# Quads 5 to 23 of an attention kernel: the turning of q and k moved from a transposing transfer to 32x32 blocks on VectorE and plain transfers

## The chip, the cores and the metric

The kernel runs on one core of a Trainium2 chip. The metric is the device time of one execution in microseconds (us). Two runs of the kernel before took 372.81 and 373.34 us, a median of 373.07 us.

## The reference

Attention with a squared ReLU in place of a softmax, and then a two-layer network on its output:

```python
# q, k, v: (8, 12, 448, 64): batch, heads, sequence S, head width D
scores = (1 / np.sqrt(D)) * np.matmul(q, k.transpose(0, 1, 3, 2))
attn = np.maximum(scores, 0.0) ** 2 / S
attn_out = np.matmul(attn, v)
x = attn_out.transpose(0, 2, 1, 3).reshape(B * S, H * D)     # 3584 x 768
h = x @ w_in                                                 # 768 -> 2048
g = np.maximum(h, 0.0) + alpha * np.minimum(h, 0.0)
out = g @ w_out                                              # 2048 -> 768, float32
```

Inputs and the output are float32 in HBM; the kernel computes its products in bf16 and accumulates in float32.

## The kernel before, in words

**Tiles.** Four heads of one batch element make a quad, so there are 3 quads in each of 8 batch elements, 24 in all (n = 0 to 23). The 448 rows of a head are held as 64 partitions of 7 rows (row = 7*pp + j). `load_qk` (L111) brings q and k of a quad by one transfer each, issued on GpSimd's queue (POOL), which casts to bf16: partitions are (head of a pair, pp), and the free dimension holds two pairs, 7 rows and 64 columns. `load_v` (L120) does the same for v. Three buffers hold raw q and raw k, six hold v.

**Turning.** The scores contract over the 64 columns, so these must come to lie on partitions. Quads 0 to 4 are turned on TensorE by `turn_pe` (L175). Quads 5 to 23 are turned by `turn_dma` (L188): two copies (L195), on ScalarE (ACT) or VectorE (DVE) by the letter that the plan gives, reorder q and k into a tile `perm`, and one transposing transfer, issued on SyncE's queue (SP, L197), writes the tile `T`. In quads 5, 7 and 8 a part of `w_mix` serves as `perm`, since it is not yet filled. There is one other `perm` buffer and four `T` buffers.

**Scores.** `score_mm` (L203) makes the scores of one quad and one j: four matmuls of 64x64 tiles (two row groups r, two column groups c), each with 448 moving columns, into a pair of the 8 PSUM banks. `relu` (L214, on ACT at L218 or DVE at L220) brings them to SBUF, `square` (L223, ACT at L229 or DVE at L231) squares them, `attnv` (L233) multiplies with v in 28 matmuls of 64x64 tiles (L241), and its result goes to `xT` (L253 or L255).

**The network.** `f1_mm` (L273) makes one of 16 units of the first layer for one batch element: six matmuls of 448 columns (L275) into one bank. `f1_out` (L279) lets ACT write `neg` (L281, two buffers) and DVE write `gT` from `neg` and the bank (L282). The second layer is made in `f2` (L290) or, for pairs of row blocks, in the class `Pair`, whose seven products p1 to p7 (L335) take mixed weights `w_mix` (made by DVE at L313) and mixed activations `S` (DVE, L331). DVE adds up results of these (L340), and results are stored by transfers on SP (L291); six `o` buffers hold them.

**Order.** Nothing is scheduled by a planner: the plan is a string of words written out by hand, one call after the other, which each engine then follows in order. `cA` or `cD` makes one score step with its relu on ACT or DVE; `s0D` squares; `v` is attnv; `f` is a unit of the first layer; `p5` is a product of a pair; `dnX` turns quad n with its copies on engine X; `ln` is `land(n)`; `Lqn` loads q and k of a quad; `nX` is `prepare` (L409): turn quad n, `land(n)`, load q and k of quad n+2 and v of quad n+1. Quads 5 to 10 are turned by `d` words, 11 to 23 by `n` words (`n` alone means ACT). By the letters, quads 5, 6, 7, 8, 12, 15, 18 and 20 are copied on DVE, the other eleven on ACT.

`land` (L417) is one copy of a single element of `T[n]` on POOL. As POOL's queue runs in order, the loads behind it are not issued before `T[n]` has landed.

The engines meet at semaphores only. SP's queue holds the transposing transfers and the stores of results in the plan's order; a transfer that waits holds up those behind it.

Of the kernel before, what the change touches and what calls it, by code (L numbers as in the profile page):

```python
# [11 lines left out]
BF16 = mybir.dt.bfloat16  # L12
# [2 lines left out]

PP = 64
NJ = 7


@with_exitstack  # L20
def kernel(
# [10 lines left out]
    nc = tc.nc  # L32
    B, H, S, D = q.shape
    d_model, d_ff = moe_w_in.shape
    assert H * D == d_model and S == PP * NJ and D == 64 and H % 4 == 0 and B % 2 == 0
    NG = H // 4
# [7 lines left out]
    ctx.enter_context(tc.manual_schedule())  # L44
    singles = ctx.enter_context(tc.tile_pool(name="singles", bufs=1))
    raw_pool = ctx.enter_context(tc.tile_pool(name="raw", bufs=3))
    v_pool = ctx.enter_context(tc.tile_pool(name="v", bufs=6))
    perm_pool = ctx.enter_context(tc.tile_pool(name="perm", bufs=1))
    T_pool = ctx.enter_context(tc.tile_pool(name="T", bufs=4))
    rl_pool = ctx.enter_context(tc.tile_pool(name="rl", bufs=6))  # L50
    at_pool = ctx.enter_context(tc.tile_pool(name="at", bufs=10))
    xT_pool = ctx.enter_context(tc.tile_pool(name="xT", bufs=2))
    neg_pool = ctx.enter_context(tc.tile_pool(name="neg", bufs=2))
    o_pool = ctx.enter_context(tc.tile_pool(name="o", bufs=6))
    u_pool = ctx.enter_context(tc.tile_pool(name="u", bufs=2))
    S_pool = ctx.enter_context(tc.tile_pool(name="S", bufs=4))
    ps_pool = ctx.enter_context(tc.tile_pool(name="ps", bufs=1, space=bass.MemoryType.PSUM))
# [9 lines left out]
    landed = singles.tile([1, 1], BF16)  # L67
# [12 lines left out]
    def take_pair():  # L80
        lo = min((0, 2, 4, 6), key=lambda i: (max(taken[i], taken[i + 1]), i))
        take(lo, 2)
        return psum[:, lo:lo + 2]
# [25 lines left out]
    raw, vraw = {}, {}  # L109

    def load_qk(n, names="qk"):  # L111
        b, g = divmod(n, NG)
        for name in names:
            src = q if name == "q" else k
            t = raw_pool.tile([128, 2, NJ, D], BF16, tag=name, name=f"{name}raw")
            flat = src[b].rearrange("(m two) (pp j) d -> (two pp) m (j d)", two=2, j=NJ)
            nc.gpsimd.dma_start(out=t.rearrange("p m j d -> p m (j d)"), in_=flat[:, 2 * g:2 * g + 2])
            raw[(n, name)] = t

    def load_v(n):  # L120
        b, g = divmod(n, NG)
        t = v_pool.tile([128, 2, NJ, D], BF16, tag="v", name="vraw")
        flat = v[b].rearrange("(m two) (pp j) d -> (two pp) m (j d)", two=2, j=NJ)
        nc.gpsimd.dma_start(out=t.rearrange("p m j d -> p m (j d)"), in_=flat[:, 2 * g:2 * g + 2])
# [12 lines left out]
    def load_w_out(h, lo=0, hi=KF, step=4):  # L137
        for lo in range(lo, hi, step):
            nc.gpsimd.dma_start(out=w_out_sb[:, lo:lo + step, COLS[h][0]:COLS[h][1]], in_=w_out_v[:, lo:lo + step, COLS[h][0]:COLS[h][1]])

    FIRST = 4
    flat0 = {name: src[0].rearrange("(m two) (pp j) d -> (two pp) m (j d)", two=2, j=NJ)[:, :2]
             for name, src in (("q", q), ("k", k))}
# [10 lines left out]
    for lo, hi, eng in ((0, 4, nc.sync), (4, NJ, nc.scalar)):  # L154
        t = o_pool.tile([128, 2, (hi - lo) * D], F32, tag="o", name=f"qfirst{lo}")
# [10 lines left out]

    warm(31)
    load_qk(1)
    load_v(0)
    load_qk(2)  # L170
    load_v(1)


    T = {}
# [13 lines left out]
    def turn_dma(n, eng="A"):  # L188
        if n in (5, 7, 8):
            w = w_mix[2 + n % 2].rearrange("p k c -> p (k c)")[:, :4 * NJ * D]  # L190
            p = w.rearrange("p (a j s d) -> p a j s d", a=2, j=NJ, s=2)
        else:
            p = perm_pool.tile([128, 2, NJ, 2, D], BF16, tag="perm", name="perm")
        for i, name in enumerate("qk"):
            (nc.vector.tensor_copy if eng == "D" else nc.scalar.copy)(p[:, i], raw.pop((n, name)).rearrange("p s j d -> p j s d"))  # L195
        t = T_pool.tile([128, 2, NJ, 128], BF16, tag="T", name="T")
        nc.sync.dma_start_transpose(out=t.rearrange("p a j c -> p (a j) c"),  # L197
                                    in_=p.rearrange("p a j s d -> p (a j s d)"))
        T[n] = t


    att, xT = {}, {}
# [1 line left out]
    def score_mm(n, j):  # L204
        ps = take_pair()
        t = T[n]
        for r in range(2):
            for c in range(2):
                nc.tensor.matmul(ps[64 * c:64 * c + 64, r, :S],  # L209
                                 t[64 * r:64 * r + 64, 1, j, 64 * c:64 * c + 64],  # L210
                                 t[64 * r:64 * r + 64, 0, :, 64 * c:64 * c + 64],
                                 start=True, stop=True)
        return ps

    def relu(ps, eng):
# [45 lines left out]
    def chunk(eng):  # L261
        if stream:
            n, j = stream.pop(0)
            late.append((n, j, relu(score_mm(n, j), eng)))
# [143 lines left out]
    def prepare(n, eng="A"):  # L408
        if n < NQ:  # L409
            turn_dma(n, eng)  # L410
            land(n)
        if n + 2 < NQ:
            load_qk(n + 2)
        if n + 1 < NQ:
            load_v(n + 1)

    def land(n):  # L417
        nc.gpsimd.tensor_copy(landed, T[n][:1, 0, 0, :1])  # L418

    class Walk:  # L420

# [11 lines left out]
        def step(self, w):  # L433
# [41 lines left out]
            elif c == "w":  # L475
                i, half = int(rest[0]), int(rest[1])
                weight_mix(i, 4 * half, 4 * half + 4)
            elif c == "g":
                f2(self.b // 2, int(rest[0]), int(rest[1]))
            elif c == "n":  # L480
                prepare(self.quad, rest or "A")
                self.quad += 1
            elif c == "x":
                cast0(int(rest[0]), int(rest[1]), rest[2])
            elif c == "t":
                turn_pe(int(rest[0]), ((rest[1], int(rest[2]), int(rest[3]), rest[4]),))
            elif c == "d":
                turn_dma(int(rest[:-1]), rest[-1])
            elif c == "l":
                land(int(rest))  # L490
            elif c == "L":
                n = [int(x) for x in rest[1:].split(",")]
                {"q": load_qk, "v": load_v, "i": load_w_in, "o": load_w_out}[rest[0]](*n)
            elif c == "i":
                warm(int(rest))
            elif c == "y":
                bank = min(range(8), key=lambda i: (taken[i], i))
                for _ in range(int(rest)):
                    nc.tensor.matmul(psum[:, bank, :128], idle, idle, start=True, stop=True)
            elif c == "z":  # L500
                two_queues.append(1)
            elif c == "b":
                nc.vector.tensor_scalar(beta_sb, alpha_sb, -1.0, 1.0, ALU.mult, ALU.add)
# [48 lines left out]
```

## Time and profile before

The profiled execution took 373.07 us, the same as the median; its span, from the first instruction to the last, is 371.3 us, so 1.8 us lie around it. The granted TensorE clock was 1.00 throughout.

| engine | busy us | share of the span | instructions |
|---|---|---|---|
| TensorE matmuls (PE) | 363.6 | 98% | 3105 |
| TensorE weight loads (PEld) | 197.5 | 53% | 3105 |
| VectorE (DVE) | 278.0 | 75% | 445 |
| ScalarE (ACT) | 274.7 | 74% | 406 |
| GpSimd (POOL) | 71.7 | 19% | 120 |

| transfers | number | us from issue to landing, median |
|---|---|---|
| transposing, from `perm` | 16 | 4.0 |
| transposing, from `w_mix` | 3 | 6.3 |
| loads of raw q / raw k / v, 224 KB each | 23 / 23 / 24 | 4.1 / 5.3 / 6.5 |
| stores of 96 KB on SP | 91 | 2.2 |

How to read it: an engine's busy time is the time in which at least one of its instructions ran. The page also has groups of instructions (line, engine, operation, output and inputs, count; then busy time, mean duration of one in ns, and the idle time just before them with what ended it), a chain of work followed back from the last instruction, and, when asked, a timeline (start in us, duration in us, engine, line, and how many instructions are merged in the row). A row that merges several instructions gives the time from the first one's start to the last one's end. Rows of DVE overlap by some 0.08 us, since one instruction begins while the one before it drains; so the step from start to start is 0.53 us where the duration is 0.61 us.

### The profile page before, as it was taken

Reading aid. Unit: us, or ns where it says so; the run is one execution under the profiler, and the core shown is the slowest. Engines: PE = TensorE matmul, PEld = TensorE weight load, DVE = VectorE, ACT = ScalarE, POOL = GpSimd, SP = SyncE. Lnnn points to the kernel's source line nnn. Section 1 sums busy time; section 2 is a strip of 40 time slices with the busy share of each in tenths; the row PEclk is TensorE's granted clock in tenths of the full one; section 3 lists DMA queues with packets and bytes.
Section 4 is the critical chain, followed back from the end, with each engine's and each line's share of the span. In section 5 each row is a group of like instructions: output and inputs, shape, how many; then the busy total and the mean of one; then the engine's idle time right before and its main releaser. Section 6 shows DMA issues by size and latency. Waiting matters only on the chain.

```text
span 371.3 us, 7894 instructions
## 1 busy us (share of the span) xinstructions
PE 363.6 (98%) x3105; PEld 197.5 (53%) x3105; DVE 278.0 (75%) x445; ACT 274.7 (74%) x406; POOL 71.7 (19%) x120
## 2 busy tenths in 40 slices
PE   8799999999999999999999999999999999999995
PEld 6454564444554565545555455554555455555563
DVE  3989988885968989566887768888749667856653
ACT  5998676877997678885997859967699866964400
POOL 8566150304211222022020220202200000000000
PEclk9999999999999999999999999999999999999999
DMA  9999989999999868455882659727646201220024
GB/s 143 188 203 202 199 135 191 153 160 167 180 171 150 123 96 163 92 89 90 160 144 64 99 80 168 144 56 121 111 89 134 49 2 43 65 65 0 0 64 108
DMA packets 73557, 43.29 MB, mean 117 GB/s; under 512 B 40368, under 2 KB 73008, under 8 KB 73520
## 3 DMA queue, kind: packets, MB, share of 16 engines
q0 software_dynamic: 27136, 22.58, 42.0%
q1 hardware_dynamic: 45712, 19.61, 25.9%
q10 hardware_dynamic: 672, 0.59, 0.5%
q8 instruction: 24, 0.39, 0.4%
q14 instruction: 13, 0.11, 0.1%
HBM read 45.62 MB, written 11.01 MB: 153 GB/s over the span
## 4 chain that ended last, share of the span: by engine, by line
PE 94%; DVE 2%; ACT 2%; issue 1%; ACTq 0%
PE psum L275 38%; PE psum L335 30%; PE psum L241 9%; PE psum L209 9%; PE psum L300 6%; PE psum L183 1%; PE psum L165 1%; DVE gT L282 1%; ACT rl L218 1%; ACT xT L253 1%; ACT neg L281 1%; DVE w_mix L195 1%; DVE T L186 0%; DVE at L231 0%; DVE osb L340 0%
## 5 line engine op out<-in xcount | busy, mean ns | idle before, releaser
L275 PE MATMUL psum<-xT,w_in_sb 128*128 128x448 bf16 x768 | 150.4, 353 | 0.2 <-DVE gT L282 0.2
L282 DVE SCALAR_TENSOR_TENSOR gT<-neg,beta_sb,psum 128x448 bf16<-128x448 f32 x128 | 85.3, 679 | 43.4 <-ACT neg L281 42.1
L218 ACT ACTIVATE rl<-psum 128x896 bf16<-128x896 f32 x128 | 111.2, 925 | 6.7 <-PE psum L209 4.7
L275 PEld LDWEIGHTS <-w_in_sb 128*128 128x128 bf16 x768 | 73.4, 98 | 73.0 <-issue 6.8
L281 ACT ACTIVATE neg<-psum 128x448 f32<-128x448 f32 x128 | 68.5, 547 | 41.0 <-PE psum L275 32.7
L231 DVE TENSOR_TENSOR at<-rl 128x896 bf16<-128x896 bf16 x105 | 62.2, 620 | 0.5 <-ACT rl L218 0.2
L229 ACT ACTIVATE at<-rl 128x896 bf16<-128x896 bf16 x63 | 58.6, 952 | 0.3
L335 PEld LDWEIGHTS <-S 128*128 128x128 bf16 x384 | 36.7, 98 | 28.4 <-issue 5.3
L335 PE MATMUL psum<-w_mix,S 128*128 128x384 bf16 x288 | 49.8, 326 | 0.2
L220 DVE TENSOR_SCALAR rl<-psum 128x896 bf16<-128x896 f32 x40 | 43.2, 1086 | 8.7 <-PE psum L209 8.1
L209 PE MATMUL psum<-T 64*64 64x448 bf16 x672 | 45.9, 357 | 2.0 <-DVE T L186 1.0
L418 POOL COPY landed<-T 1x1 bf16<-1x1 bf16 x18 | 3.3, 181 | 206.1 <-DMA T<-perm 182.9
L335 PEld LDWEIGHTS <-gT 128*128 128x128 bf16 x296 | 28.3, 98 | 20.2 <-issue 1.8
L241 PE MATMUL psum<-at,vraw 64*64 64x448 bf16 x672 | 36.6, 350 | 0.0
L335 PE MATMUL psum<-w_out_sb,gT 128*128 128x384 bf16 x192 | 34.0, 326 | 0.0
L340 DVE TENSOR_TENSOR osb<-psum,u 128x384 f32<-128x384 f32 (+2 forms) x37 | 20.2, 547 | 12.6 <-PE psum L335 8.2
L209 PEld LDWEIGHTS <-T 64*64 64x64 bf16 x672 | 17.4, 105 | 22.7 <-issue 14.8
L241 PEld LDWEIGHTS <-vraw 64*64 64x64 bf16 x672 | 21.2, 106 | 11.9 <-issue 2.9
L300 PE MATMUL psum<-w_out_sb,gT 128*128 128x256 bf16 (+1 forms) x128 | 22.0, 326 | 0.1
L255 DVE TENSOR_SCALAR xT<-psum 128x448 bf16<-128x448 f32 x24 | 14.9, 622 | 8.9 <-PE psum L241 8.3
L253 ACT ACTIVATE xT<-psum 128x448 bf16<-128x448 f32 x24 | 13.3, 556 | 9.1 <-PE psum L241 8.7
L356 ACT COPY osb<-psum 128x384 f32<-128x384 f32 x12 | 5.8, 480 | 17.4 <-PE psum L335 17.4
(45 smaller groups left out, 242.0 us busy)
## 6 DMA issues: line engine op xcount, KB each, us to landing
out_dram<-osb SPq DMA_DIRECT2D x91, 96.0 KB, 2.2
vraw<-in_v_dram POOLq DMA_DIRECT2D x24, 224.0 KB, 6.5
qraw<-in_q_dram POOLq DMA_DIRECT2D x23, 224.0 KB, 4.1
kraw<-in_k_dram POOLq DMA_DIRECT2D x23, 224.0 KB, 5.3
w_in_sb<-in_moe_w_in_dram POOLq DMA_DIRECT2D x16, 192.0 KB, 8.0
w_out_sb<-in_moe_w_out_dram POOLq DMA_DIRECT2D x4, 512.0 KB, 9.5
w_out_sb<-in_moe_w_out_dram POOLq DMA_DIRECT2D x4, 256.0 KB, 8.8
out_dram<-osb SPq DMA_DIRECT2D x8, 128.0 KB, 3.2
```

What stands on the lines that cost most here:

```text
L209: nc.tensor.matmul(ps[64 * c:64 * c + 64, r, :S], t[64 * r:64 * r + 64, 1, j, 64 * c:64 * c + 64], t[64 * r:64 * r + 64, 0, :, 64 * c:64 * ...
L218: nc.scalar.activation(rl, ps[:, :, :S], ACTF.Relu)
L220: nc.vector.tensor_scalar(rl, ps[:, :, :S], 0.0, None, ALU.max)
L229: nc.scalar.activation(a, rl, ACTF.Square)
L231: nc.vector.tensor_tensor(a, rl, rl, ALU.mult)
L241: nc.tensor.matmul(ps[64 * s:64 * s + 64, r, :S], vv[64 * r:64 * r + 64, s, j, :], a[64 * r:64 * r + 64, s], start=(j == 0), stop=(j == NJ ...
L275: nc.tensor.matmul(ps, w_in_sb[:, km // 2, km % 2, bass.ts(ff, 128)], xT[b][:, km // 2, km % 2, :], start=(km == 0), stop=(km == KM - 1))
L281: nc.scalar.activation(neg, ps, ACTF.Relu, scale=-1.0)
L282: nc.vector.scalar_tensor_tensor(gT[:, ff, (b % 2) * S:(b % 2) * S + S], neg, beta_sb[:, ff:ff + 1], ps, ALU.mult, ALU.add)
L300: nc.tensor.matmul(ps, gT[:, ff, bass.ts(c, 128)], w_out_sb[:, ff, first_col + lo:first_col + hi], start=(ff == 0), stop=(ff == KF - 1))
L335: nc.tensor.matmul(ps, left[:, i], right[:, i], start=(start and i == 0), stop=(i == KH - 1), skip_group_check=not start)
L340: nc.vector.tensor_tensor(t, ps, u, ALU.add)
```

## The change

Only quads 5 to 23 are touched; quads 0 to 4 are turned as before.

- `load_qk`: for these quads q and k come by two transfers each, one for a pair of heads, of 64 partitions. The pair lies on the partition halves, the head of the pair in the free dimension.
- `turn_dma`: the two copies become two VectorE transposes of 32x32 blocks (128 x 896 elements each). They are always on VectorE; the letter of the plan has no effect any more. The transposing transfer becomes eight plain transfers on SP, each of 32 partitions by 2 runs of 448 elements (896 bytes a run, 56 KB in all), which bring the four combinations of partition group and column half, for each of two pairs, to their places.
- `score_mm`: for these quads each 64x64 tile is split in two tiles of 64 rows by 32 columns, so eight matmuls of 448 columns take the place of four. Two tiles share the moving operand; it is now read in runs of 32 elements.
- `land` does nothing.
- Buffers: v 6 to 5, o 6 to 5, `perm` 1 to 2.

```diff
+PE_TURNED = 4
...
-    v_pool = ctx.enter_context(tc.tile_pool(name="v", bufs=6))
-    perm_pool = ctx.enter_context(tc.tile_pool(name="perm", bufs=1))
+    v_pool = ctx.enter_context(tc.tile_pool(name="v", bufs=5))
+    perm_pool = ctx.enter_context(tc.tile_pool(name="perm", bufs=2))
...
-    o_pool = ctx.enter_context(tc.tile_pool(name="o", bufs=6))
+    o_pool = ctx.enter_context(tc.tile_pool(name="o", bufs=5))
...
-            flat = src[b].rearrange("(m two) (pp j) d -> (two pp) m (j d)", two=2, j=NJ)
-            nc.gpsimd.dma_start(out=t.rearrange("p m j d -> p m (j d)"), in_=flat[:, 2 * g:2 * g + 2])
+            if n <= PE_TURNED:
+                flat = src[b].rearrange("(m two) (pp j) d -> (two pp) m (j d)", two=2, j=NJ)
+                nc.gpsimd.dma_start(out=t.rearrange("p m j d -> p m (j d)"), in_=flat[:, 2 * g:2 * g + 2])
+            else:
+                flat = src[b].rearrange("(m two) (pp j) d -> m pp two (j d)", two=2, j=NJ)
+                for m in range(2):
+                    nc.gpsimd.dma_start(out=t[64 * m:64 * m + 64].rearrange("p w j d -> p w (j d)"), in_=flat[2 * g + m])
...
     def turn_dma(n, eng="A"):
         if n in (5, 7, 8):
             w = w_mix[2 + n % 2].rearrange("p k c -> p (k c)")[:, :4 * NJ * D]
-            p = w.rearrange("p (a j s d) -> p a j s d", a=2, j=NJ, s=2)
+            x = w.rearrange("p (i b f c) -> p i b f c", i=2, b=2, c=32)
         else:
-            p = perm_pool.tile([128, 2, NJ, 2, D], BF16, tag="perm", name="perm")
+            x = perm_pool.tile([128, 2, 2, 2 * NJ, 32], BF16, tag="perm", name="perm")
         for i, name in enumerate("qk"):
-            (nc.vector.tensor_copy if eng == "D" else nc.scalar.copy)(p[:, i], raw.pop((n, name)).rearrange("p s j d -> p j s d"))
+            rows = raw.pop((n, name)).rearrange("p w j d -> p (w j) d")
+            nc.vector.transpose(x[:, i].rearrange("p b f c -> p f b c"), rows.rearrange("p f (b c) -> p f b c", b=2))
         t = T_pool.tile([128, 2, NJ, 128], BF16, tag="T", name="T")
-        nc.sync.dma_start_transpose(out=t.rearrange("p a j c -> p (a j) c"),
-                                    in_=p.rearrange("p a j s d -> p (a j s d)"))
-        T[n] = t
+        z = t.rearrange("p i j c -> p i (j c)").rearrange("p i (a f c) -> p i a f c", a=2, c=32)
+        for m in range(2):
+            for a in range(2):
+                for b in range(2):
+                    nc.sync.dma_start(out=z[64 * m + 32 * b:64 * m + 32 * b + 32, :, a],
+                                                      in_=x[64 * m + 32 * a:64 * m + 32 * a + 32, :, b])
+        T[n] = z
...
-                nc.tensor.matmul(ps[64 * c:64 * c + 64, r, :S],
-                                 t[64 * r:64 * r + 64, 1, j, 64 * c:64 * c + 64],
-                                 t[64 * r:64 * r + 64, 0, :, 64 * c:64 * c + 64],
-                                 start=True, stop=True)
+                if n <= PE_TURNED:
+                    nc.tensor.matmul(ps[64 * c:64 * c + 64, r, :S],
+                                     t[64 * r:64 * r + 64, 1, j, 64 * c:64 * c + 64],
+                                     t[64 * r:64 * r + 64, 0, :, 64 * c:64 * c + 64],
+                                     start=True, stop=True)
+                else:
+                    moving = t[64 * r:64 * r + 64, 0, :, NJ * c:NJ * c + NJ].rearrange("p a j i -> p j a i")
+                    for a in range(2):
+                        lo = 64 * c + 32 * a
+                        nc.tensor.matmul(ps[lo:lo + 32, r, :S],
+                                         t[64 * r:64 * r + 64, 1, a, NJ * c + j], moving,
+                                         start=True, stop=True)
...
     def land(n):
-        nc.gpsimd.tensor_copy(landed, T[n][:1, 0, 0, :1])
+        pass
```

In the built program the changed kernel has 38 transposes on VectorE and 16 fewer copies there, 22 fewer copies on ScalarE, 152 plain transfers on SP in place of 19 transposing ones, 38 more loads on POOL, 532 more matmuls with as many weight loads, and 68 more instructions on VectorE and 65 more on TensorE that only wait for a semaphore.

## The prediction

> **What bounds the kernel now.** I read, in this order: busy times, the chain of work, the groups, the waits, and the timeline wherever q and k are turned.
>
> ```profile
> PE 363.6 (98%) x3105; PEld 197.5 (53%) x3105; DVE 278.0 (75%) x445; ACT 274.7 (74%) x406; POOL 71.7 (19%) x120
> PE 94%; DVE 2%; ACT 2%; issue 1%; ACTq 0%
> ```
>
> TensorE is the bound: 98% busy, and 94% of the chain. So work taken off other engines gains almost nothing, and work put on another engine costs only where TensorE then comes to wait for it. The groups give the prices:
>
> ```profile
> L209 PE MATMUL psum<-T 64*64 64x448 bf16 x672 | 45.9, 357 | 2.0 <-DVE T L186 1.0
> L195 ACT COPY perm<-kraw 128x896 bf16<-128x896 bf16 x11 | 10.5, 957 | 0.0
> L195 DVE COPY perm<-qraw 128x896 bf16<-128x896 bf16 x5 | 3.1, 612 | 0.0
> L220 DVE TENSOR_SCALAR rl<-psum 128x896 bf16<-128x896 f32 x40 | 43.2, 1086 | 8.7 <-PE psum L209 8.1
> L255 DVE TENSOR_SCALAR xT<-psum 128x448 bf16<-128x448 f32 x24 | 14.9, 622 | 8.9 <-PE psum L241 8.3
> L282 DVE SCALAR_TENSOR_TENSOR gT<-neg,beta_sb,psum 128x448 bf16<-128x448 f32 x128 | 85.3, 679 | 43.4 <-ACT neg L281 42.1
> T<-perm SPq DMA_TRANSPOSE x16, 4.0
> out_dram<-osb SPq DMA_DIRECT2D x91, 96.0 KB, 2.2
> POOL landed L418 <- DMA T<-perm: 182.9, 16, 19.4
> ```
>
> The first is the score matmul, the next two a copy on ACT and on DVE, then three DVE rows that price a pass, then the two kinds of SP transfer, and the wait that `land` makes. Two stretches of the timeline show what a longer DVE costs. First, quads 6, 7 and 8:
>
> ```profile
> 61.14 0.61 DVE L195 COPY perm<-qraw 128x896 bf16<-128x896 bf16 x1
> 62.37 2.03 DVE L282 SCALAR_TENSOR_TENSOR gT<-neg,beta_sb,psum 128x448 bf16<-128x448 f32 x3
> 65.38 3.97 DVE L282 SCALAR_TENSOR_TENSOR gT<-neg,beta_sb,psum 128x448 bf16<-128x448 f32 x6
> ...
> 69.27 0.61 DVE L195 COPY w_mix<-qraw 128x896 bf16<-128x896 bf16 x1
> 70.32 0.67 DVE L282 SCALAR_TENSOR_TENSOR gT<-neg,beta_sb,psum 128x448 bf16<-128x448 f32 x1
> 71.05 2.24 PE L275 MATMUL psum<-xT,w_in_sb 128*128 128x448 bf16 x11 [0.17 <-DVE gT L282]
> ```
>
> DVE has no gap worth naming here, and at 71.05 TensorE already waits for its last gT. Second, quad 13, whose copies are now on ACT:
>
> ```profile
> 137.17 0.68 DVE L331 TENSOR_TENSOR S<-S,gT 128x1024 bf16<-128x1024 bf16 x1
> 137.77 0.55 DVE L340 TENSOR_TENSOR osb<-psum,u 128x384 f32<-128x384 f32 x1
> 138.75 0.81 PE L335 MATMUL psum<-w_out_sb,S 128*128 128x384 bf16 x4
> ```
>
> In the plan `p5 n p4 p3`, product p3 adds into the bank that this L340 reads. L340 ends at 138.32, p3 starts at 138.75: 0.41 us of slack after the semaphore. The changed order puts both transposes between L331 and L340.
>
> **The change part by part.**
>
> *Transposes on DVE.* No row shows one. L255 and L220 give (1.086-0.622)/448 = 1.04 ns per element and 0.16 us fixed. From below, the copy of the same tile, 0.61 us, which is about half of that pace. From above, two L282 of 448 elements, 1.36 us, the slowest pace of a DVE row on such tiles. I take 1.09 us, L220's, whose count it shares and whose pace of one element per lane and step I expect of a block transpose. DVE starts its next instruction 0.08 us early, so a pair blocks it for 2.02 us, against 1.06 for a pair of copies. "VectorE: DVE Perf Modes" (The three transpose paths) of the Trainium skill states 311 ns for 128x128 bf16; scaled from that with L220's slope, 896 columns are an estimated 1.11 us, which moves the sum by 0.3 us.
>
> *What of this reaches TensorE.* Quads with copies on DVE get 0.96 us more, those with copies on ACT 2.02. From each place I follow DVE's row in its order to the first TensorE instruction that waits for it; its start less the end of what it waits for, gaps on the way counted, is the slack. Stall = added - gap before the next DVE instruction - slack:
> - 5: 0.96-0.13-0.23 = 0.60 (the last gT before the f2 product at 46.56).
> - 6, 7, 8, one run up to 71.05: 2.88-0.18-0.27 = 2.43.
> - 9 and 10: DVE is full from 88.6 to 104.8 (w_mix, S, squares), so they add up: 4.04-0.93 = 3.11, the last part at 105.76.
> - 11: 2.02-0.79 = 1.23 (gT before 119.06).
> - 13: 2.02-0.41 = 1.61.
> - 16 and 19, the same `p5 n p4 p3`: 2.02-0.10-0.52 = 1.40 each (p3 at 184.79 and 230.74).
> - 21: 2.02-1.13 = 0.89. 22: 2.02-0.88-0.72 = 0.42.
> - 12, 15, 18, 20: 0.96 against 1.27 to 3.49 of slack, nothing. 14, 17, 23: DVE sits idle 1.43 us for ACT's neg, which ACT without its copies gives earlier; 2.02-1.51 = 0.51 against 0.75, nothing.
>
> Sum 13.1 us. With copies' pace (1.06 and 0) the same lines give 2.8; with 1.36 us (pair 2.56, +0.54 a quad) 13 quads add 7.0 and the four just spared 1.1, so 21.2.
>
> *68 more waiting instructions on DVE*, 0.021 to 0.050 us each by the rows of L195: 1.4 to 3.4 us, of which about half lies at the places above; I take 1.0, range 0 to 2.
>
> *ACT loses 22 copies*, 21 us. TensorE waits for ACT in few places (2% of the chain), so I book nothing beyond quads 14, 17 and 23.
>
> *Scores on 64x32 tiles.* A group of four matmuls takes 9% of the span / 168 = 0.20 us, and in the trace's records of a burst groups start 0.189 us apart, matmuls within a group 3.5 ns apart: the four run side by side. From below, eight also do, and a group stays at 0.189. From above, only four do: 0.379. I take the first: row groups and column groups are independent now, and 28 ns of issue fit in 189. A burst gets 4 x 3.5 = 14 ns longer; 53 bursts belong to quads from 5 on: 0.7 us. The 65 waits on TensorE come in front of scores whose T landed long ago, behind queued matmuls: nothing, at most 65 x 0.05 = 3.3. "TensorE: Matmul & The Clock Gate" (Measured speedup vs the span model) states 2.38 times for three column tiles, 79% of ideal, which speaks against this; by it a group would take an estimated 0.24 us and the sum would be 6.6 us more.
>
> *Eight SP transfers for one.* SP spends 0.47 to 0.59 us per store of L291, so 3.8 to 4.7 us for eight, and the last lands 2.2 us (96 KB stores) to 4.6 us (the page's 64 KB stores) later. T thus lands 6 to 9.3 us after the transposes, against 4.0 after the copies. In the records T leads its scores by 13 to 24 us from quad 11 on, 6.7 to 10.7 in 7 to 10: covered; if not, each us late is a us of TensorE. Quad 5: transposed at 44.2, landed 50.2 to 53.5, needed at 52.86 plus its 0.6: nothing. Quad 6: transposed at 63.2, landed 69.2 to 72.5, needed at 68.88: a stall of 0.3 to 3.6, but DVE works on through it, so it covers the 2.43 of that run; I add nothing, at most 1.2. Stores queue behind: quad 16's, issued from 184.27, move to about 189; with five o buffers the first reuse is at 196.35: covered. "DMA: Bandwidth & Descriptors" (Rules for kernel authors) says to coalesce, since under 64 KB a transfer is mostly overhead; at its fixed 2 us each, taken in a row, T6 would land near 79 and the sum grow by an estimated 8 us. L291's rows show issues 0.5 us apart and landings that overlap.
>
> *Loads and `land`.* 38 more POOL issues of 0.62 to 0.72 us, 24 to 27 us on an engine 19% busy. Without `land` POOL's 206 us of waiting go and loads are held only by buffers; q and k come earlier, which nobody waits for; they can collide with T of quads 5 and 6, inside the bounds above. With five v buffers, v of n+1 waits for attnv of n-4, which ended before that load's old issue.
>
> Sum: 13.1+1.0+0.7 = 14.8. The profiled execution took 373.07, its span 371.3 with 1.8 around it, equal to the median: 373.1+14.8 = 387.9, so 388 us.
>
> **The rivals.**
> - *Not slower: a transpose is as quick as a copy.* Place: the DVE rows above; price 2.8+0.5+0.7 = 4.0, so 377. For it: same tile, same type. Against: copies run at twice L220's pace. It decides below about 0.77 us a transpose, where the sum, on a line between the two, is 7.5 (2%).
> - *Column tiles run four at a time.* 133 groups x 0.19 = 25.3 on TensorE, behind which some DVE delay hides: 398 to 413, say 406. For it: no row has four column groups. Against: two run freely.
> - *Transfers bound.* With the longest L291 issue, 1.42 us, eight take 11.4 and land 4.6 later: T5 stalls 7, T6 10, T9 4.7, in place of 2.4 at 6 to 8: about 405. [...]
> - *Faster, over 2%:* TensorE's busy 363.6 plus its 5 us start leave no room; no view shows a mechanism.
>
> **How the numbers follow.** Forecast 0.58 (alone 381 to 397), quick transposes 0.20, column tiles 0.12, transfers 0.07, faster 0.03. The range 376 to 402 holds the first two and leaves out most of the rest, about 0.2. Two per cent, 365.6 to 380.5, is about what a measurement of this kernel can tell from no change. Faster 0.03; same 0.20 + 0.02 of the forecast's edge = 0.22; slower 0.56+0.12+0.07 = 0.75.
>
> **What would show it.** Right: transposes near 1.09 us; score groups still 0.19 us apart; DVE near 310 us busy, ACT near 254; new TensorE idle time before L275, L300 and L335 ended by gT (L282) and osb (L340), most of it between 60 and 145 us and around p3 of quads 16 and 19; none ended by transfers after quad 6. Wrong: transposes of 0.6 or 1.8 us, score groups of 0.38 us, or TensorE waiting for T.

## The result and the profile after

The changed kernel takes 394.49 us (median of 2 runs, 394.11 to 394.87) against 373.07 us before: a ratio of 1.057, with a 95% interval of 1.052 to 1.063. It is 21.4 us slower, where 14.8 us were forecast. Its profiled execution took 394.87 us, with a span of 393.1 us against 371.3.

The page of the changed kernel: busy times, the clock in 40 slices, and the chain of work.

```profile
PE 372.5 (95%) x3633; PEld 195.9 (50%) x3637; DVE 304.9 (78%) x467; ACT 258.8 (66%) x384; POOL 86.4 (22%) x140
PEclk9999999889999999999999999999999999999999
PE 72%; DVE 12%; SPq 6%; DMA 4%; issue 3%; ACT 1%; DVEq 0%; ACTq 0%
```

DVE holds 12% of the chain where it held 2%, and transfers with SP's queue another 10% where there were none. TensorE's busy time also grew, by 8.9 us, in part because it runs more slowly in slices 8 and 9, where the clock's digit is 8. DVE's 304.9 us and ACT's 258.8 are near the 310 and 254 that were forecast. The groups, with every releaser of the idle time, and the two rows of transfers:

```profile
L229 PE MATMUL psum<-T 64*32 64x448 bf16 x1064 | 38.0, 358 | 7.1 <-DMA T<-perm 5.4 <-DVE rl L239 1.0 <-DMA T<-w_mix 0.4
L202 DVE STREAM_TRANSPOSE perm<-qraw 128x896 bf16<-128x896 bf16 x16 | 17.7, 1104 | 0.0
L202 DVE STREAM_TRANSPOSE perm<-kraw 128x896 bf16<-128x896 bf16 x16 | 17.1, 1069 | 0.0
L354 PE MATMUL psum<-w_out_sb,S 128*128 128x384 bf16 x96 | 17.5, 326 | 4.8 <-DVE osb L359 4.8
```

```profile
T<-perm SPq DMA_DIRECT2D x128, 56.0 KB, 3.6
T<-w_mix SPq DMA_DIRECT2D x24, 56.0 KB, 5.3
```

A transpose takes 1.07 to 1.10 us; 1.09 was taken. The p3 products (L354, once L335) now wait 4.8 us for osb, as forecast. The 5.4 us that the scores wait for T were not. The timeline shows where they are:

```profile
64.70 6.00 SPq L208 DMA_DIRECT2D T<-perm  x8
...
65.65 4.70 PE L294 MATMUL psum<-xT,w_in_sb 128*128 128x448 bf16 x24
73.25 0.37 PE L229 MATMUL psum<-T 64*32 64x448 bf16 x4 [2.90 <-DMA T<-perm]
76.12 1.31 PE L229 MATMUL psum<-T 64*32 64x448 bf16 x20 [2.50 <-DMA T<-perm]
```

This is quad 6. SP issues its eight transfers from 64.7 to 70.7, one every 0.63 to 0.69 us but for one gap of 1.47; in the records the last is issued at 70.1 and lands at 75.9, 5.8 us later. The forecast had T6 whole by 69.2 to 72.5. The same stretch in windows (busy time of PE, PEld, DVE, ACT and POOL; then clock, DMA share and GB/s):

```profile
70.00:73.00 3.00, 0.36 (x2) 0.00 (x0) 2.92 (x5) 2.00 (x4) 1.90 (x3) 1.00 1.24 227
77.00:82.00 5.00, 5.00 (x25) 1.96 (x14) 1.30 (x2) 2.81 (x4) 1.21 (x2) 0.50 1.28 215
82.00:87.00 5.00, 5.00 (x49) 2.41 (x46) 2.91 (x5) 3.21 (x6) 0.00 (x0) 0.99 0.29 68
```

The DMA engines are full (a share over 1) until 82 us, then nearly empty: loads that used to be held back now run beside T6. And after TensorE's idle time its clock is 0.50, in the trace from 75.24 to 82.07: 25 matmuls in 5 us, against 49 in the next 5. The two waits are 5.4 us. At the half clock TensorE was busy for about 6.0 of the 6.8 us, so an estimated 3.0 us went there.

To see where time is lost, I matched TensorE's weight loads (those of the scores left out) of each kernel with those of the kernel before, one by one, and read how far they lag. These are the lags gained in each stretch, in us; times are those of the kernel before, and the letters those of the experiments below.

| kernel | to 50 (quad 5) | 50-57 (T5) | 57-85 (6-8) | 85-106 (9, 10) | 106-125 (11) | 125-150 (13) | 150-196 (16) | 196-243 (19) | 243-290 (21, 22) | end |
|---|---|---|---|---|---|---|---|---|---|---|
| after | 0.4 | 1.0 | 8.4 | 3.0 | 1.5 | 1.7 | 1.8 | 1.9 | 1.6 | 21.6 |
| e2, tiles alone | 0.2 | 0.3 | 0.0 | 0.3 | 0.3 | 0.1 | 0.5 | 0.6 | 0.4 | 2.9 |
| e5, loads held | 0.2 | 0.3 | 3.7 | 3.0 | 1.5 | 1.7 | 1.8 | 1.9 | 1.7 | 15.9 |
| e6, before without `land` | 0.1 | 7.5 | 0.8 | 0 | 0 | 0 | 0 | 0 | 0 | 8.4 |
| e7, 5 to 8 as before | 0 | 0 | 0 | 2.9 | 1.5 | 1.7 | 1.8 | 1.9 | 1.7 | 11.7 |
| e8, half the transposes | -0.3 | 1.2 | 5.6 | 1.0 | 0.6 | 0.7 | 0.8 | 0.9 | 0.4 | 11.2 |
| e9, two issuers | 0.7 | 0.3 | 2.6 | 3.0 | 1.5 | 1.7 | 1.8 | 1.9 | 1.7 | 15.4 |

The first column holds the start too, which differs from run to run by -0.4 to 0.2 us; quad 5 alone is the step from 40 to 50 us, 0.5 in the changed kernel.

### The profile page after: what moved, and what is told of

Read it like the earlier page. It is cut to its first block, busy times and chain, and to the rows that moved or that the text cites. A ratio compares the mean times of both kernels' runs of the same rounds, so it can differ in the third digit from the quotient of the medians.

```text
span 393.1 us, 9204 instructions
## 1 busy us (share of the span) xinstructions
PE 372.5 (95%) x3633; PEld 195.9 (50%) x3637; DVE 304.9 (78%) x467; ACT 258.8 (66%) x384; POOL 86.4 (22%) x140
## 4 chain that ended last, share of the span: by engine, by line
PE 72%; DVE 12%; SPq 6%; DMA 4%; issue 3%; ACT 1%; DVEq 0%; ACTq 0%
PE psum L294 30%; PE psum L354 24%; PE psum L260 7%; PE psum L229 6%; SPq L208 5%; DVE perm L202 3%; DVE at L250 3%; DMA T<-perm 2%; PE psum L319 2%; DVE gT L301 2%; DMA T<-w_mix 1%; DVE S L350 1%; PE psum L171 1%; DVE rl L239 1%; PE psum L221 1%
## 5 line engine op out<-in xcount | busy, mean ns | idle before, releaser
L294 PE MATMUL psum<-xT,w_in_sb 128*128 128x448 bf16 x768 | 152.6, 356 | 0.4 <-DVE gT L301 0.4
L301 DVE SCALAR_TENSOR_TENSOR gT<-neg,beta_sb,psum 128x448 bf16<-128x448 f32 x128 | 84.0, 675 | 36.1 <-ACT neg L300 34.9
L294 PEld LDWEIGHTS <-w_in_sb 128*128 128x128 bf16 x768 | 74.2, 99 | 75.0 <-issue 9.7
L300 ACT ACTIVATE neg<-psum 128x448 f32<-128x448 f32 x128 | 68.9, 546 | 55.3 <-PE psum L294 39.6
L123 POOL DMA_DIRECT2D qraw<-in_q_dram x38 | 22.6, 600 | 137.3 <-DVE perm L202 129.8
L354 PEld LDWEIGHTS <-S 128*128 128x128 bf16 x384 | 36.4, 98 | 32.7 <-issue 10.0
L354 PE MATMUL psum<-w_mix,S 128*128 128x384 bf16 x288 | 49.9, 326 | 0.0
L229 PE MATMUL psum<-T 64*32 64x448 bf16 x1064 | 38.0, 358 | 7.1 <-DMA T<-perm 5.4
L354 PEld LDWEIGHTS <-gT 128*128 128x128 bf16 x296 | 28.3, 98 | 20.2 <-issue 1.8
L354 PE MATMUL psum<-w_out_sb,gT 128*128 128x384 bf16 x192 | 34.0, 326 | 0.0
L130 POOL DMA_DIRECT2D vraw<-in_v_dram x24 | 17.7, 739 | 51.7 <-PE psum L260 49.7
L229 PEld LDWEIGHTS <-T 64*32 64x32 bf16 x1064 | 12.7, 90 | 29.3 <-issue 26.9
L260 PEld LDWEIGHTS <-vraw 64*64 64x64 bf16 x672 | 19.4, 106 | 14.7 <-issue 6.5
L123 POOL DMA_DIRECT2D kraw<-in_k_dram x38 | 22.9, 614 | 3.3 <-DMA vraw<-in_v_dram 1.4
```

The source lines that it names most:

```text
L123: nc.gpsimd.dma_start(out=t[64 * m:64 * m + 64].rearrange("p w j d -> p w (j d)"), in_=flat[2 * g + m])
L229: nc.tensor.matmul(ps[lo:lo + 32, r, :S], t[64 * r:64 * r + 64, 1, a, NJ * c + j], moving, start=True, stop=True)
L260: nc.tensor.matmul(ps[64 * s:64 * s + 64, r, :S], vv[64 * r:64 * r + 64, s, j, :], a[64 * r:64 * r + 64, s], start=(j == 0), stop=(j == NJ ...
L294: nc.tensor.matmul(ps, w_in_sb[:, km // 2, km % 2, bass.ts(ff, 128)], xT[b][:, km // 2, km % 2, :], start=(km == 0), stop=(km == KM - 1))
L300: nc.scalar.activation(neg, ps, ACTF.Relu, scale=-1.0)
L301: nc.vector.scalar_tensor_tensor(gT[:, ff, (b % 2) * S:(b % 2) * S + S], neg, beta_sb[:, ff:ff + 1], ps, ALU.mult, ALU.add)
```

## The experiments

**Is it `land`? (e1)** The theory was that the loads which `land` no longer holds back collide with T6; the rival, that eight issues in a row are simply late.

```diff
-        pass
+        nc.gpsimd.tensor_copy(landed, T[n][:1, 0, 0, 0, :1])
```

> The changed kernel with land put back: the loads behind it wait again until T of a quad has landed. Theory (the loads that are no longer held share the transfer engines with T of quads 5 and 6): T6's eight transfers land 2 to 4 us after their issue, not 5.3 to 6.6; TensorE's loss at quads 5 to 8 shrinks from 10.0 us to the 3 to 4 us that VectorE alone makes, the clock stays at 1.00, and the time is 388 us (386 to 390). Rival (eight issues 0.64 us apart, after a longer VectorE pass, are what makes T6 late): T6 still lands 5 us or more after TensorE asks for it, and the time stays at 392 to 395 us.

Measured: 393.65 us, ratio 1.053 [1.047, 1.059]. The number is the rival's, but the edit did not do what it was meant to. The element read lies in what the first of the eight transfers writes, so the loads were released when that one landed, at 65.7. The records of T6 show both cases in one row: its first four transfers landed 2.0 us after their issue, the other four, now beside the loads, after 3.6, 5.5, 6.5 and 6.8 us. So the test was made again.

**Hold the loads until the last transfer has landed (e5)**, by reading what the eighth writes:

```diff
-    landed = singles.tile([1, 1], BF16)
+    landed = singles.tile([128, 1], BF16)
...
-        pass
+        nc.gpsimd.tensor_copy(landed[96:97], T[n][96:97, 0, 1, 0, :1])
```

> The changed kernel, with GpSimd's one-element copy put back in front of the next quads' loads, this time reading an element that the last of the eight transfers writes. Theory (the loads that are no longer held back share the DMA engines with T6's transfers): all eight of T6 land about 2 us after their issue, the last by 70.5; TensorE's idle time before quad 6's scores falls from 5.4 us to under 1, its clock stays at 1.00, and of the 9.6 us that quads 5 to 8 lose, some 3 stay (VectorE's transposes): 387 to 389. Rival (eight issues of 0.64 us on SP's queue make T6 late by themselves, loads or no loads): 392 to 395, with the last transfers still landing 5 us or more after their issue. Second rival: held loads come too late for quads 7 and 8, and TensorE waits there for qraw or v: over 392 with a wait on the loads.

Measured: 388.61 us, ratio 1.041 [1.040, 1.043]; with the loads held the loss is 5.9 us less, nearly all of it at quads 5 to 8. TensorE's timeline and the windows of this kernel:

```profile
69.28 0.37 PE L229 MATMUL psum<-T 64*32 64x448 bf16 x4
71.35 0.75 PE L229 MATMUL psum<-T 64*32 64x448 bf16 x20 [1.70 <-DMA T<-perm]
```

```profile
70.00:73.00 3.00, 1.65 (x25) 0.82 (x26) 2.92 (x5) 2.43 (x5) 1.50 (x3) 0.97 0.33 80
73.00:77.00 4.00, 3.67 (x13) 1.38 (x11) 2.21 (x4) 2.30 (x5) 1.61 (x3) 0.60 1.00 155
```

The DMA share in 70 to 73 falls from 1.24 to 0.33, T6's last six transfers land in 2.0 to 2.2 us (its first two, still beside a load of `w_out`, in 4.1 and 3.6), and 5.4 us of waiting become 1.7. Two details missed: the last landed at 71.1, not 70.5, and in the profiled run the clock still fell, to 0.50 from 72.82 to 76.23. It was that run alone: it took 389.30 us at a mean clock of 0.995, the other three 388.46 to 388.71 at 0.999 to 1.000. The time fits the collision; the rival's 392 to 395 does not.

**Only `land` removed, in the kernel before (e6).**

```diff
     def land(n):
-        nc.gpsimd.tensor_copy(landed, T[n][:1, 0, 0, :1])
+        pass
```

> The kernel before with only one line of the change: GpSimd's one-element copy, which holds the next loads until a T has landed, is taken out; the transposing transfer stays, and so do score tiles, pools and copies. If that copy is what kept transfers and loads apart, T5's or T6's transposing transfer now meets the loads, as T5's did when quads 5 to 8 went the old way without it: 6 to 9 us longer, 379 to 382. Rival (the loads matter only to the eight plain transfers): 372 to 374.

Measured: 382.59 us, ratio 1.025 [1.023, 1.027]. One line of the change costs 9.4 us by itself, a little more than the 6 to 9 expected. T5's transposing transfer, issued at 43.3, lands at 58.7, in place of 49.6 in the kernel before. In the profile, the row of the transfers, once 6.3 us, and TensorE's timeline:

```profile
T<-w_mix SPq DMA_TRANSPOSE x3, 15.4
```

```profile
58.77 1.33 PE L209 MATMUL psum<-T 64*64 64x448 bf16 x12 [5.76 <-DMA T<-w_mix]
```

**Quads 5 to 8 the old way (e4, e7).** In e4 these quads keep copies, transposing transfer, whole loads and 64x64 tiles, without `land`; e7 is e4 with `land(n)` for n up to 8.

```diff
-PE_TURNED = 4
+PE_TURNED = 8
...
+        if n <= PE_TURNED:
+            return turn_old(n, eng)
...
     def land(n):
-        pass
+        if n <= PE_TURNED:
+            nc.gpsimd.tensor_copy(landed, T[n][:1, 0, 0, :1])
```

The last three lines are in e7 only; `turn_old` is `turn_dma` of the kernel before.

> The changed kernel with quads 5 to 8 turned the old way: two copies on VectorE, one transposing transfer, 64x64 tiles; land still does nothing. Theory (quads 5 to 8 cost 10.0 us, of it about 3 on VectorE and 7 by T6's late landing with its clock drop): if the one transposing transfer lands in time beside the loads, 384 to 385 us; if it too collides with them, TensorE waits for T6 and the time is 387 to 390 us. Rival (the loss at quads 5 to 8 comes from elsewhere, the tiles or the buffers): 392 to 395 us.

> The changed kernel with quads 5 to 8 turned in the old way and with the one-element copy in front of the loads for n up to 8, so that those quads are as before in everything; quads 9 to 23 are as changed. By place: the changed kernel loses 9.6 us by quad 8 and 12 us behind it; if the two parts are independent, this is 373.2 + 11.9 = 385 (384 to 386). Rival (what comes late in quads 9 to 22 hides behind the delay of quads 5 to 8): over 388.

e4 measured 393.55 us, ratio 1.052 [1.047, 1.058], above both times that the theory named. The number is the rival's, but the trace does not show the rival: the loss went from T6 to T5, whose transposing transfer met the unheld loads as in e6. TensorE's timeline of e4:

```profile
58.83 1.33 PE L236 MATMUL psum<-T 64*64 64x448 bf16 x12 [5.89 <-DMA T<-w_mix]
```

e7 measured 384.98 us, ratio 1.032 [1.030, 1.033], the 385 expected. Up to 85 us it does not lag at all, and behind that it lags place by place as the changed kernel does. The two parts add up, and nothing of the one hides in the other. As e7 keeps the changed kernel's buffers, these cost nothing up to quad 8, and e4's rival falls.

**What is VectorE's (e3, e8).** e3 is the kernel before with all 38 copies on DVE, a smaller dose of the same kind (1.06 us more at eleven quads). e8 is the changed kernel with only k transposed, and q copied into the same buffer.

```diff
-            (nc.vector.tensor_copy if eng == "D" else nc.scalar.copy)(p[:, i], raw.pop((n, name)).rearrange("p s j d -> p j s d"))
+            nc.vector.tensor_copy(p[:, i], raw.pop((n, name)).rearrange("p s j d -> p j s d"))
```

```diff
+            if name == "q":
+                (nc.vector.tensor_copy if eng == "D" else nc.scalar.copy)(x[:, i].rearrange("p b f c -> p f b c"), rows.rearrange("p f (b c) -> p f b c", b=2))
+            else:
                 nc.vector.transpose(x[:, i].rearrange("p b f c -> p f b c"), rows.rearrange("p f (b c) -> p f b c", b=2))
```

> The kernel before with all 38 copies on VectorE, none on ScalarE; nothing else changed. It gives VectorE 1.06 us more at each of eleven quads. Theory (added time less the slack up to the first TensorE instruction that waits): 1.2 at quads 9 and 10, 0.3 at 11, 0.65 at 13, 0.35 at 16 and at 19, nothing elsewhere: 2.8 us, 376 us (375 to 377). Rival (ScalarE's 21 us of relief pays it back): 371 to 373 us. Rival (VectorE has no slack, all of it shows): 11.7 us, 385 us.

> The changed kernel with only k's half transposed on VectorE; q's half is a plain copy into the same buffer, on the engine that copied it before (so q's blocks are not transposed and the scores are not the reference's; the same tiles, transfers and matmuls run). Theory (the loss at quads 9 to 22 is VectorE's added time less the slack of each place): 1.08 us less at each place: quads 16 and 19 fall from 1.5 to 0.4 us, 13 from 1.4 to 0.3, 11 from 1.3 to 0.2, 9 and 10 together from 3.1 to 0.9, 21 and 22 to 0; about 8 us in all, 386 (384.5 to 387.5). Rival (the loss there is the latency of the eight transfers or of more semaphores): the places keep their loss, 392 to 395.

e3 measured 376.24 us, ratio 1.007 [1.005, 1.009]: 3.0 us for the 2.8 expected, at the expected places (9 and 10 1.1; 11 0.36; 13 0.67; 16 and 19 0.37 each). e8 measured 384.76 us, ratio 1.031 [1.030, 1.033]. Its losses at 16 and 19 fell by 1.0 us each, at 13 by 1.0, at 9 and 10 by 2.0, while tiles and transfers stayed, and DVE's waiting instructions only went from 189 to 178 (121 in the kernel before). So the loss at quads 9 to 22 is DVE's added time less a slack; the latency of the transfers and the number of waits are not it.

**What is left at quads 6 to 8 (e9).** As e5, with half the transfers issued by POOL:

```diff
-                    nc.sync.dma_start(out=z[64 * m + 32 * b:64 * m + 32 * b + 32, :, a],
+                    (nc.gpsimd if m and n <= 8 else nc.sync).dma_start(out=z[64 * m + 32 * b:64 * m + 32 * b + 32, :, a],
```

> As e5_land_last (the copy in front of the loads waits for the last transfer), and of quads 5 to 8 the four transfers of the lower half (m = 1) are issued by GpSimd instead of SP, so that each queue has four. In e5_land_last T6's eight issues ran from 63.7 to 69.1 us, 0.64 apart, the last landed at 71.11, TensorE waited 1.7 us for it and then ran 73 to 77 us at a clock of 0.60. Theory (what was left there is the row of issues on one queue): T6 is whole by 69.3, the wait of 1.7 us goes and with it most of the slow clock's 1.6 us: 388.6 - 3 = 385.5 to 387. Rival (VectorE's four transposes hold quads 5 to 8 back by themselves, as forecast, 2.4 us): 387.5 to 389, with TensorE waiting there for gT, rl or at. Second rival: GpSimd's issues cost more than SP's and T6 comes no earlier: 388 to 390.

Measured: 388.54 us, ratio 1.042 [1.040, 1.044], the same as e5: my theory fell. T6 was whole by 68.9, and TensorE waited for DVE instead, as its timeline in e9 shows:

```profile
70.64 0.56 PE L229 MATMUL psum<-T 64*32 64x448 bf16 x12 [0.46 <-DVE gT L301]
71.40 0.37 PE L229 MATMUL psum<-T 64*32 64x448 bf16 x4 [0.20 <-DVE gT L301]
71.99 1.30 PE L294 MATMUL psum<-xT,w_in_sb 128*128 128x448 bf16 x6 [0.22 <-DVE gT L301]
74.57 5.65 PE L294 MATMUL psum<-xT,w_in_sb 128*128 128x448 bf16 x29 [1.28 <-DVE gT L301]
```

These are 2.2 us, and the stretch lags by 2.6 us: with the transfers out of the way, the 2.43 us that were forecast for DVE at this place appear. The wait for T in e5 lay in front of the same delay. The whole program won nothing in the medians; the 0.5 us in the profiled lag is no more than the half clock of e5's profiled run.

**The tiles by themselves (e2):** the kernel before, quads from 5 on scored on 64x32 tiles.

```diff
-                nc.tensor.matmul(ps[64 * c:64 * c + 64, r, :S],
-                                 t[64 * r:64 * r + 64, 1, j, 64 * c:64 * c + 64],
+                for a in range(2) if n > 4 else (None,):
+                    lo, w = (64 * c, 64) if a is None else (64 * c + 32 * a, 32)
+                    nc.tensor.matmul(ps[lo:lo + w, r, :S],
+                                     t[64 * r:64 * r + 64, 1, j, lo:lo + w],
```

> The kernel before with one edit: the scores of quads 5 to 23 run on 64x32 tiles; copies, transposing transfers and land stay. Theory (eight tiles run side by side, a burst is 14 ns longer): groups 0.19 us apart and 373.8 us (373 to 374.5). Rival (column tiles keep only 79% of their pace): groups of 0.24 us and 380 us. Rival (four at a time): 398 us.

Measured: 375.58 us, ratio 1.005 [1.003, 1.008]; 2.3 us instead of 0.6. TensorE's timeline at one of the bursts (a burst is a run of score matmuls with no other between them), first of the kernel before, then of e2:

```profile
176.76 0.38 PE L209 MATMUL psum<-T 64*64 64x448 bf16 x4
176.97 1.49 PE L241 MATMUL psum<-at,vraw 64*64 64x448 bf16 x28
178.30 0.55 PE L209 MATMUL psum<-T 64*64 64x448 bf16 x8
178.78 2.77 PE L335 MATMUL psum<-w_mix,S 128*128 128x384 bf16 x16
```

```profile
178.10 0.38 PE L211 MATMUL psum<-T 64*32 64x448 bf16 x8
178.42 1.52 PE L243 MATMUL psum<-at,vraw 64*64 64x448 bf16 x28
179.87 0.57 PE L211 MATMUL psum<-T 64*32 64x448 bf16 x16
180.37 0.82 PE L337 MATMUL psum<-w_mix,S 128*128 128x384 bf16 x4
```

From the first row's start to the last's it is 2.02 us before and 2.27 us in e2. The records of all 53 bursts, matched one by one, show where the time goes. The 19 bursts with no attnv beside them take as long as before, up to the matmul behind them: their groups start 200 and 189 ns apart (before 213 and 189), and the next matmul 305 ns after the last group (before 292). So eight tiles do run side by side, and a burst is not longer. Of the 17 bursts ahead of an attnv, 13 lose 0.10 us (from the last group to the first attnv matmul 313 ns instead of 213, or 302 instead of 189); of the 17 behind one, 8 lose 0.12 us, since the first group starts 289 ns after attnv's last group instead of 189. The other 13 lose next to nothing, as a step beside them was longer before. Together that is 2.3 us, all of it at a change between scores and attnv. Before, both had 64x64 tiles; the changes to and from 128x128 matmuls, which were there before as well, cost no more than they did. "TensorEngine Tiling (Array Packing)" (Key Properties) of the Trainium skill says "Changing tiling mode (not just tile) drains the TensorE", which agrees with these transitions; the price comes from here. The changed kernel shows the same: 312 and 289 ns.

**Can ScalarE's relief be spent? (e10, e11)** e10 is e7 with 12 squares of the plan on ACT (two of these words stand in a plan that runs three times). e11 is e10 with the turns of 13, 16 and 19 behind p3. An excerpt of that plan, first for e10, then for e11:

```diff
-vDA s1D s0D cAA p6 s0D pd p7 n cA rc s1A cAA s0D s0A p5 p4 rb p3 cAAD
+vDA s1D s0A cAA p6 s0A pd p7 n cA rc s1A cAA s0D s0A p5 p4 rb p3 cAAD
```

```diff
-p7 n cA rc s1A cAA s0D s0A p5 p4 rb p3 cAAD
+p7 cA rc s1A cAA s0D s0A p5 p4 rb p3 n cAAD
```

> As e7_old_5_to_8_held (quads 5 to 8 as before), and 12 squares of the scores (0.62 us each on VectorE, 0.95 on ScalarE) that stand close ahead of the turns of quads 9, 10, 11, 13, 16, 19, 21 and 22 go from VectorE to ScalarE, which the change relieved of two copies of 0.95 us at each of these places. Theory (the loss at quads 9 to 22 is VectorE's time): each place wins up to 0.62 us for each square moved: 16, 19: 1.5 to 0.3; 11 and 13: 1.3 and 1.4 to 0.2; 21, 22: 0.9 and 0.6 to 0; 9 and 10: 2.9 to 1.7; 7 to 8 us less, 385.0 to 378 (377 to 380.5); not below the kernel before, since the score tiles' 1.6 to 2.3 us and a rest at 9 and 10 stay. Rival (ScalarE has no room at these places; its square of 0.95 us ends later than VectorE's would have): 383 to 388, with TensorE's or VectorE's waits on ScalarE.

> As e10_squares_to_act, and the turns of quads 13, 16 and 19 (n in the plan) go behind p3, that is, behind the additions into osb and u that TensorE's p3 matmuls wait for; before, the two transposes stood right between the u and the osb of one chain (186.3 to 192.4 us: u, transposes, S, square, osb, then TensorE after 1.20 us idle). Theory (what counts is VectorE's work between an input that TensorE delivers and the output that TensorE needs; squares that stand before that stretch gain nothing, and that is why e10 won nothing at 16 and little at 13 and 19): the losses of 1.2, 1.6 and 1.2 us at 13, 16 and 19 nearly go, 382.2 to 378.3 - 379.8. Rival (VectorE is full there whatever the order, so the transposes push the relu and xT behind p3 back as much): 381 to 383, with new TensorE waits just behind p3.

e10 measured 382.2 us, ratio 1.025 [1.022, 1.028]: 2.8 us less than e7 (2.6 in the profiled lag), not 7. DVE and TensorE around p3 of quad 16 in e10:

```profile
186.31 0.56 DVE L374 TENSOR_TENSOR u<-psum,u 128x384 f32<-128x384 f32 x1
187.14 1.11 DVE L217 STREAM_TRANSPOSE perm<-qraw 128x896 bf16<-128x896 bf16 x1 [0.27 <-issue]
...
190.27 1.01 DVE L374 TENSOR_TENSOR osb<-psum,u 128x384 f32<-128x384 f32 x2
```

```profile
190.87 1.46 PE L369 MATMUL psum<-w_out_sb,S 128*128 128x384 bf16 x8 [1.20 <-DVE osb L374]
```

DVE now has idle time ahead of the transposes, yet TensorE waits as long (1.09 us in e7). The moved squares stood ahead of `u`, which waits for TensorE's product; only work between that input and osb delays osb. Where a moved square stood inside such a stretch, it helped (lag gained, tiles included: 11 1.5 to 0.6; 9 and 10 2.9 to 2.2; 21 1.2 to 0.7).

e11 measured 383.24 us, ratio 1.029 [1.026, 1.031]; against e10 nothing is won (the two medians, 382.2 and 383.2, have overlapping ranges). The p3 waits of these three quads are gone, and others of 0.97 to 1.02 us stand some 5 us further on (for rl at 16 and 19, for u at 13). DVE's and TensorE's timeline of e11 at quad 16:

```profile
192.56 1.07 DVE L217 STREAM_TRANSPOSE perm<-kraw 128x896 bf16<-128x896 bf16 x1
193.55 1.05 DVE L254 TENSOR_SCALAR rl<-psum 128x896 bf16<-128x896 f32 x1
```

```profile
189.55 1.46 PE L369 MATMUL psum<-w_out_sb,S 128*128 128x384 bf16 x8
...
194.66 0.38 PE L244 MATMUL psum<-T 64*32 64x448 bf16 x8 [0.98 <-DVE rl L254]
```

My theory fell and the rival holds: the relu that stood behind the osb frees the scores' banks, and it is now late by what the osb was late before. No version came near the kernel before.

## Why the prediction was right in sign and 6.6 us short

*Right, and tested.* The transposes cost what was taken, 1.09 us. The slack method holds: quad 5 was forecast at 0.60 and gave 0.5; less e2's share of tiles in each stretch, 9 and 10 gave 2.7 (3.11), 11 1.3 (1.23), 13 1.6 (1.61), 16 and 19 1.3 each (1.40), 21 and 22 together 1.3 (1.31). The sum without 6 to 8 is 10.0 for a forecast of 10.7. Quads 6 to 8 gave 2.6 (2.43) in e9, once the transfers were out of the way. Here, for instance, are DVE and TensorE of the changed kernel at quad 13, with both transposes between S and osb:

```profile
151.51 0.68 DVE L350 TENSOR_TENSOR S<-S,gT 128x1024 bf16<-128x1024 bf16 x1
152.11 1.10 DVE L202 STREAM_TRANSPOSE perm<-qraw 128x896 bf16<-128x896 bf16 x1
153.13 1.07 DVE L202 STREAM_TRANSPOSE perm<-kraw 128x896 bf16<-128x896 bf16 x1
154.13 0.52 DVE L359 TENSOR_TENSOR osb<-psum,u 128x384 f32<-128x384 f32 x1
```

```profile
154.70 0.49 PE L354 MATMUL psum<-w_out_sb,S 128*128 128x384 bf16 x2 [1.39 <-DVE osb L359]
```

*The step that failed* is "they can collide with T of quads 5 and 6, inside the bounds above", together with quad 6's "at most 1.2". The collision was seen and not priced. The bounds came from landings of SP's stores, medians over the whole span. Unheld, the loads push the landing of T6 from 2.0 to between 5.3 and 6.6 us, which TensorE waits for, and then its clock drops, which stood in no term. T5 loses 0.8 us (1.0 less 0.25 for tiles) and quads 6 to 8 5.8 us (8.4 less 2.6): 6.5 us in all. e5 gives 5.9 of it back, and e6 shows the same line of the change costing 9.4 us on its own. That q and k "come earlier, which nobody waits for" was true, and beside the point: what `land` did was to keep loads and transfers apart.

That the collision is about as large as the whole shortfall is in part luck, since the other errors nearly cancel: the tiles were put 1.9 us too low, the waiting instructions up to 1.0 too high and the places 0.5 too high. So is it that 394.5 us lies within the stated 376 to 402: the largest terms that the prediction priced above 388 were transposes of 1.36 us and tiles four at a time, and neither came. Of the signs named, the one for "wrong", TensorE waiting for T, did come.

*The term for the tiles* was too small, and for another reason than its 0.7: bursts did not get longer at all, yet 2.3 us were measured (2.6 in the profiled lag beyond the start). The view was right on the point in dispute, that eight tiles run side by side. It missed the 0.10 to 0.12 us at changes between 64x32 and 64x64, since scores and attnv had one shape before.

*The waiting instructions'* 1.0 us was not isolated. The measured stalls of the places contain whatever they cost, and come to 10.0 + 2.6 = 12.6, where 13.1 were forecast without them; so no run shows this term. With 6.5 for the collision and 2.6 for the tiles the parts make 21.7 of the 21.6 us in the profiled lag.

*Two side sums* of the prediction are slightly off: its list holds 12 quads and not 13, so the slowest transposes would give 20.7 us and not 21.2, and copies' pace gives 3.0 and not 2.8. The forecast itself does not use them.

*The rivals.* "Transfers bound" named T6 and was right that T can be late, by a mechanism that no run shows: T6's issues stayed 0.63 to 0.69 us apart but for one of 1.47, where the rival took 1.42 for all, and T9 was never late. Quick transposes and column tiles four at a time are excluded by the durations and by e2.

The covers held elsewhere: quads 12, 15, 18 and 20, and 14, 17 and 23, gave nothing beyond tiles, and no score waits for a transfer behind quad 6.

## What to carry to other kernels

An instruction that does nothing but wait may be the schedule of the DMA engines: before removing one, ask which transfers it holds back and which wanted transfer they would meet, and price that by a landing time taken from a stretch in which the engines are already full. An added instruction on an engine off the critical path is charged from the last input that it gets from the bound engine to the first output that the bound engine waits for; taking work away outside that stretch does not pay it back. Price a new matmul shape by its neighbours in the order too: the change of shape has its own cost.

## What the hardware showed that was not expected

- A transfer of 56 KB within the core's memory, issued by SP every 0.64 us, lands after 2.0 us when no load runs beside it (e1, e5) and after 5.0 to 6.8 us when loads do (T5 and T6 of the changed kernel, and e1, where the first that met them took 3.6); T5's transposing transfer goes from 6.3 to 15.4 us (e6). In e9 four transfers of T7, issued by POOL, took 10.1 to 10.5 us.
- In every trace here TensorE's clock is 1.00 or 0.50; the 0.78, 0.60 and 0.99 of the windows are means. It changes only on steps of 3.41 us, counted in each run from the moment it first reached 1.00, so a stretch at 0.50 within the work lasts 3.41 us (e5, e8) or 6.83 us (the changed kernel, e1, e4, e6). Within the work it fell six times, each time behind a step in which TensorE had been idle for at least 1.70 us (1.70 in e5, 3.04 in the changed kernel); no step at full clock with 1.48 us or less was followed by it, and e9's four waits make at most 1.22 us in a step. At the half clock less was enough: in the changed kernel a step with 0.88 us of idle time was followed by a second one at 0.50. "TensorE: Matmul & The Clock Gate" (What's actually happening) of the Trainium skill puts the half clock after an idle window of about 3.4 us; the length of the step agrees, but 1.70 us of idle time in it sufficed here. What exactly is counted stays open: near the end of e3 a step with 1.97 us of idle time was not followed by the half clock.
- A change between matmuls of 64x32 and 64x64 tiles costs 0.10 to 0.12 us where no longer step covers it (e2); before, the two kinds had one shape and followed one another without it.
